# A two-layer gated MLP on one core: lo parts moved from GpSimd to VectorE, row sums spread over the groups

## The chip, the core and the metric

The kernel runs on one core of a Trainium2 chip. The metric is the device time of one execution in microseconds; three runs of the kernel before gave a median of 1682.23 us (1680.01 to 1683.55). One further execution was taken with the hardware profiler; all rows below come from it.

The engines are named as in the profile: PE is TensorE's matmul, PEld its weight load, DVE is VectorE, ACT is ScalarE, POOL is GpSimd, SP is SyncE (which issues the DMAs).

## The reference

An attention with a small memory comes first, and its output x (4608 tokens, 512 features) goes through two MLPs, all in float32:

```python
x = _attn_ref(q, k, v, phi)                     # reshaped to 4608 x 512
g = np.maximum(0.01 * (h := x @ w_in), h);  x = g @ w_out           # first MLP, d_ff 2048
gate = 1.0 / (1.0 + np.exp(-(x @ w_gate)))      # second MLP, d_ff 1536
val = x @ w_val
out = gate * val @ w_out
```

The change touches the second MLP alone, which takes the second half of the time.

## The kernel before

**Number format.** A float32 operand is held as two parts of a shorter type for TensorE: hi, a rounded copy made by ScalarE, and lo, the rest (operand minus hi), made by a subtraction on VectorE or GpSimd. A product of two such operands is three matmuls: hi*hi, hi*lo and lo*hi.

**Tiling of the second MLP.** Tokens are taken in five *pairs* of blocks: four pairs of 2 x 512 tokens and one of 2 x 256 (`PAIRS`). The 12 chunks of 128 hidden features are taken in three *thirds* of four chunks (index `th`), so there are 15 thirds in all, 12 full and 3 short ones. A third consists of four *groups* in the order gate, value, gate, value (indices `j` and `val` of `m2_group`), and then of the output products (`m2_out`). So in a third there is one place where a value group is followed directly by a gate group; behind the second value group stand the output products.

**A group.** Two blocks of tokens by two chunks of features are multiplied by the seven-product scheme of Winograd: seven products, k = 0 to 6, each of six matmuls of 512 columns, into three PSUM banks: x (k = 0, 3), y (k = 1, 4, 6) and z (k = 2, 5). A later product of a bank adds to what is in it, so it may start only when the earlier content has been read. The reads, in order:

- k=0: ScalarE copies x to `tmp` (L839); k=1: VectorE adds y to it (L844); k=2: ScalarE copies z (L849).
- k=3: the first result (f,t) = (0,0) is in x; k=4: VectorE reads y (L858), adds the copy of z (L859), result (1,1); k=5: VectorE reads z (L863), result (0,1); k=6: VectorE reads y (L868), result (1,0).

For each result, `finish` is called. In a gate group it is a sigmoid on ScalarE (L824) into an `sg` tile. In a value group VectorE multiplies the gate with the value (L829), ScalarE casts the product row to its hi part in a `pt` tile (L831), and a subtraction makes the lo part (L833): on GpSimd, but for the result (1,0) of the last value group of a third, which is on VectorE.

**Row sums of the next pair.** The left operands of the seven products are differences of the token blocks. For each pair and each half `a` of the features there are four subtractions on VectorE (`x_sums`, L754, L755, L757, L758) from the loaded rows `xr` into `xt`. For the next pair they stand in its predecessor's second third (th = 1): four behind the first value group, four behind the second. The loads of `xr` are issued on SP's queue at the end of the first third's groups, ahead of its output products. Their hi and lo parts (L771 on ScalarE, L775 in turn on VectorE and GpSimd) are made during the output products of the last third.

**Order.** Every engine takes its instructions in the order in which the code writes them (`tc.manual_schedule`); there is no planner here. What the code writes first is first in the engine's queue, and the tile pools add the waits for data and for buffers.

Of the kernel before, what the change touches and what calls it, by code (L numbers as in the profile page):

```python
# [93 lines left out]
def tile_kernel(  # L94
# [13 lines left out]
    nc = tc.nc  # L108
# [44 lines left out]
    def f32(ap):  # L153
        return ap.bitcast(F32)
# [15 lines left out]
    class Piece:  # L170
        i = -1
# [570 lines left out]
    def x_load(n, c):  # L742
        t0, h = PAIRS[n]
        nc.sync.dma_start(out=xr[c][:, 0:2 * h], in_=x2s[:, c, t0:t0 + 2 * h])

    def x_parts(n, a):
        h = PAIRS[n][1]
        b = [xr[2 * a + e][:, i * h:(i + 1) * h] for e in range(2) for i in range(2)]
        return b, (xt[a][:, 0:h], xt[a][:, 512:512 + h], b[1], xt[2][:, a * 512:a * 512 + h])

    def x_sums(n, a, k):
        (b11, b12, b21, b22), (t1, t2, t3, t4) = x_parts(n, a)
        if k == 0:
            nc.vector.tensor_sub(t1, b12, b11)  # L754
            nc.vector.tensor_sub(t3, b22, b12)  # L755
        else:
            nc.vector.tensor_sub(t2, b22, t1)  # L757
            nc.vector.tensor_sub(t4, b21, t2)  # L758

    def x_operand(n, k, a):  # L760
        (b11, _, b21, b22), (t1, t2, t3, t4) = x_parts(n, a)
# [2 lines left out]
    def x_hi(n, k, a):  # L764
        if n == 0:
            i = 2 * k + a
            xo[k, a] = (
                wtile("win", [P, 2, 512], F32R, "xo") if i < SLOTS["win"]
                else p2[0].tile([P, 2, 512], F32R, tag="xo", name="xo", bufs=6)
            )  # L770
        nc.scalar.copy(xo[k, a][:, 0, :PAIRS[n][1]], x_operand(n, k, a))  # L771

    def x_lo(n, k, a, eng):
        t, h = xo[k, a], PAIRS[n][1]
        eng.tensor_sub(t[:, 1, :h], x_operand(n, k, a), f32(t[:, 0, :h]))  # L775

    def w_load():
        while w_free and w_next[0] < len(PAIRS) * NOPS // 2:
            m = w_next[0] % (NOPS // 2)
            t = w_at[w_next[0]] = w_free.pop(0)  # L780
            nc.sync.dma_start(out=f32(t), in_=gvs[:, 2 * m:2 * m + 2].rearrange("p o l a f -> p (o l a f)"))
            w_next[0] += 1
# [6 lines left out]
    def tmp(h):  # L789
        n_tmp[0] += 1  # L790
        return tmps[n_tmp[0] % len(tmps)][:, :h]

    sgs = {}

    def m2_group(n, th, j, val):
        h = PAIRS[n][1]
        o0 = n * NOPS + NOP * (TH * th + 2 * j + val)
        last = val and j == TH // 2 - 1  # L800

        def prod(k, bank, start):
            m, e = divmod(o0 + k, 2)
            w = w_at[m].rearrange("p (o l a f) -> p o l a f", o=2, l=2, a=2)[:, e]
            i = 0
            for a in range(2):
                x = xo[k, a]
                for l, r in ((0, 0), (1, 0), (0, 1)):

                    nc.tensor.matmul(  # L810
                        bank, w[:, l, a, :], x[:, r, :h], start=(start and i == 0), stop=(i == 5),
                        skip_group_check=not start,
                    )
                    i += 1
            if e == 1:
                w_free.append(w_at.pop(m))
                w_load()

        def sg_tile():
            return p2[0].tile([P, 512], F32, tag="sg", name="sg", bufs=5)[:, :h]  # L820

        def finish(f, t, c, psum=False):
            if not val:
                nc.scalar.activation(sgs[f, t] if psum else c, c, AF.Sigmoid)  # L824
                if not psum:
                    sgs[f, t] = c
                return
            s = sgs.pop((f, t))
            nc.vector.tensor_mul(s, s, c)  # L829
            d = pt[2 * (2 * j + f) + t]  # L830
            nc.scalar.copy(d[:, 0, :h], s)  # L831
            eng = nc.vector if last and (f, t) == (1, 0) else nc.gpsimd
            eng.tensor_sub(d[:, 1, :h], s, f32(d[:, 0, :h]))  # L833

        new = (lambda: tmp(h)) if val else sg_tile
        x = ps_h.tile([P, 512], F32, tag="h", name="ps_x")[:, :h]
        prod(0, x, True)
        s1 = tmp(h)
        nc.scalar.copy(s1, x)  # L839
        yield  # L840
        y = ps_a.tile([P, 512], F32, tag="a", name="ps_y")[:, :h]
        prod(1, y, True)
        u2 = new()
        nc.vector.tensor_add(u2, y, s1)  # L844
        yield
        z = ps_h.tile([P, 512], F32, tag="h", name="ps_z")[:, :h]
        prod(2, z, True)
        c = tmp(h)
        nc.scalar.copy(c, z)  # L849
        yield  # L850
        prod(3, x, False)
        if not val:
            sgs[0, 0] = sg_tile()
        finish(0, 0, x, True)
        yield
        prod(4, y, False)
        u3 = new()
        nc.vector.tensor_add(u3, y, s1)  # L858
        nc.vector.tensor_add(u3, u3, c)  # L859
        finish(1, 1, u3)  # L860
        yield
        prod(5, z, False)
        nc.vector.tensor_add(u2, z, u2)  # L863
        finish(0, 1, u2)
        yield
        prod(6, y, False)
        c21 = new()
        nc.vector.tensor_add(c21, y, s1)  # L868
        finish(1, 0, c21)
        yield  # L870

    def m2_out(n, th, between):
# [54 lines left out]
    with tc.manual_schedule():  # L927
# [109 lines left out]
        for group in SCHED["prologue"]:  # L1037
# [4 lines left out]
            for x in group.split():  # L1042
# [4 lines left out]
                else:  # L1047
                    n, u = x.split(".")
# [19 lines left out]
                fin()  # L1068

        early = {0: [(x_open, ())] + [(x_load, (0, c)) for c in range(KD)]}  # L1070
        for n in range(4):
            early.setdefault(3 + n, []).append((x_sums, (0, n // 2, n % 2)))
        for n in range(2 * NOP):
            early.setdefault(6 + n, []).append((x_hi, (0, n // 2, n % 2)))
            early.setdefault(7 + n, []).append((x_lo, (0, n // 2, n % 2, nc.vector)))
# [7 lines left out]
        for n in range(TH):  # L1083
            early.setdefault(18 + 2 * n, []).append((w2_load, (n, n)))
        first = m2_group(0, 0, 0, 0)
        held = None
        for i, (b, hf, fc) in enumerate(steps):
# [47 lines left out]
        for n in range(len(PAIRS)):  # L1135
            more = n + 1 < len(PAIRS)
            for th in range(NTH):
                for j in range(TH // 2):
                    for val in range(2):
                        g = m2_group(n, th, j, val)  # L1140
                        if (n, th, j, val) == (0, 0, 0, 0):
                            g = first
                        for _ in g:
                            pass
                    if more and th == 1:
                        x_sums(n + 1, j, 0)
                        x_sums(n + 1, j, 1)
                if n + 1 < len(PAIRS) and th == 0:
                    for c in range(KD):
                        x_load(n + 1, c)  # L1150
                between = []
                if more and th == NTH - 1:
                    ops = [(k, a) for k in range(NOP) for a in range(2)]
                    for i in range(0, len(ops), 2):
                        fs = [lambda o=o: x_hi(n + 1, *o) for o in ops[i:i + 2]]
                        fs += [lambda o=o, e=e: x_lo(n + 1, *o, e) for o, e in zip(ops[i:i + 2], (nc.vector, nc.gpsimd))]
                        between.append(fs)
                    for f in between.pop(0):
                        f()
                m2_out(n, th, between)  # L1160
                if n + 2 == len(PAIRS) and th == NTH - 1:
                    w_free.extend(p2[0].tile([P, 2 * PC], F32R, tag="xr", name="wt", bufs=7) for _ in xr + xt)
                    w_load()
# [30 lines left out]
```

## Time and profile before

| | |
|---|---|
| median of 3 runs | 1682.23 us |
| the profiled execution | 1682.42 us, its span 1680.6 us |
| mean granted TensorE clock | 0.987 |
| PE busy / PEld busy | 1614.4 us (96%) / 1391.9 us (83%) |
| DVE busy | 831.0 us (49%) |
| ACT busy | 679.3 us (40%) |
| POOL busy | 581.9 us (35%) |
| chain that ended last | PE 52%, DVE 5%, ACT 1%; output products (L883) 17%, products (L810) 26% |
| lo parts of the product rows (L833) | 105 on POOL, mean 1405 ns; 15 on DVE, mean 896 ns |

A busy share says how much an engine has to do over the whole span; what a change in one place is worth has to be read at that place: which engine waits there, and for which instruction. So the rows below are mostly timelines, which list an engine's instructions in order of time, with the idle time before each and what ended it.

### The profile page before, as it was taken

Reading aid. Unit: us, or ns where it says so; the run is one execution under the profiler, and the core shown is the slowest. Engines: PE = TensorE matmul, PEld = TensorE weight load, DVE = VectorE, ACT = ScalarE, POOL = GpSimd, SP = SyncE. Lnnn points to the kernel's source line nnn. Section 1 sums busy time; section 2 is a strip of 40 time slices with the busy share of each in tenths; the row PEclk is TensorE's granted clock in tenths of the full one; section 3 lists DMA queues with packets and bytes.
Section 4 is the critical chain, followed back from the end, with each engine's and each line's share of the span. In section 5 each row is a group of like instructions: output and inputs, shape, how many; then the busy total and the mean of one; then the engine's idle time right before and its main releaser. Section 6 shows DMA issues by size and latency. Waiting matters only on the chain.

```text
span 1680.6 us, 26242 instructions
## 1 busy us (share of the span) xinstructions
PE 1614.4 (96%) x9976; PEld 1391.9 (83%) x9976; DVE 831.0 (49%) x1362; ACT 679.3 (40%) x1516; POOL 581.9 (35%) x534
## 2 busy tenths in 40 slices
PE   4688999999999999999999999999999999999998
PEld 2577888989898898989988788878887888878897
DVE  6997545454454544523142555264543454264544
ACT  4654455555455555544432133232332142222332
POOL 2776343444444354433321124121321142121311
PEclk8799999999999999999999999999999999999999
DMA  9712353444445353512465375554575456546692
GB/s 295 259 44 75 104 164 112 135 145 146 133 146 170 117 165 92 168 43 78 140 193 196 92 223 190 184 177 151 161 239 163 137 171 214 167 126 201 211 392 74
DMA packets 169022, 268.59 MB, mean 160 GB/s; under 512 B 60608, under 2 KB 105664, under 8 KB 168896
## 3 DMA queue, kind: packets, MB, share of 16 engines
q1 hardware_dynamic: 168896, 266.91, 50.1%
q8 instruction: 79, 1.29, 0.3%
q14 instruction: 47, 0.39, 0.1%
HBM read 219.68 MB, written 47.19 MB: 159 GB/s over the span
## 4 chain that ended last, share of the span: by engine, by line
PE 52%; DVE 5%; issue 1%; ACT 1%; DMA 0%; DVEq 0%; ACTq 0%; SPq 0%
PE oacc L883 17%; PE ps_y L810 11%; PE ps_x L810 8%; PE ps_z L810 7%; PE acc L700 5%; PE ps_h L678 3%; DVE sg L829 2%; DVE tmp L859 1%; DVE tmp L858 1%; PE ps_vw L651 0%; DVE tmp L868 0%; DVE tmp L863 0%; ACT tmp L839 0%; DVE xt L754 0%; DVE xr L755 0%
## 5 line engine op out<-in xcount | busy, mean ns | idle before, releaser
L700 PE MATMUL acc<-gh,wo 128*128 128x288 f32 x2048 | 434.6, 304 | 0.3 <-ACT gh L160 0.3
L833 POOL TENSOR_TENSOR pt<-sg,pt 128x512 fp32r<-128x512 f32 (+1 forms) x105 | 146.0, 1405 | 639.7 <-ACT pt L831 586.5
L700 PEld LDWEIGHTS acc<-gh,wo 128*128 128x128 f32 x2048 | 326.9, 189 | 37.4 <-ACT gr L683 19.5
L161 POOL TENSOR_TENSOR gl<-gr,gh 128x288 fp32r<-128x288 f32 x250 | 221.7, 890 | 334.7 <-ACT gh L160 210.8
L700 PE MATMUL acc<-gl,wo 128*128 128x288 f32 x1024 | 304.2, 297 | 1.3 <-POOL gl L161 1.3
L883 PE MATMUL oacc<-w2t,pt 128*128 128x512 f32 x1296 | 296.3, 389 | 0.0
L883 PEld LDWEIGHTS oacc<-w2t,pt 128*128 128x128 f32 x1296 | 243.1, 188 | 50.3
L810 PE MATMUL ps_y<-xo,wt 128*128 128x512 f32 (+1 forms) x1080 | 255.1, 372 | 9.1 <-DVE sg L844 9.1
L683 ACT ACTIVATE gr<-ps_h 128x288 f32<-128x288 f32 x256 | 105.4, 412 | 327.5 <-PE ps_h L678 299.7
L810 PEld LDWEIGHTS ps_y<-xo,wt 128*128 128x128 f32 x1080 | 191.7, 190 | 45.1 <-DVE sg L844 10.8
L678 PE MATMUL ps_h<-at_hi,vw 128*128 128x288 f32 x1024 | 213.7, 297 | 8.5 <-ACT vw L160 6.6
L700 PEld LDWEIGHTS acc<-gl,wo 128*128 128x128 f32 x1024 | 193.8, 189 | 2.3 <-POOL gl L161 2.0
L678 PEld LDWEIGHTS ps_h<-at_hi,vw 128*128 128x128 f32 x1024 | 166.3, 190 | 9.6 <-ACT vw L160 7.5
L810 PE MATMUL ps_x<-xo,wt 128*128 128x512 f32 (+1 forms) x720 | 169.3, 370 | 3.2 <-ACT tmp L839 2.6
L810 PE MATMUL ps_z<-xo,wt 128*128 128x512 f32 (+1 forms) x720 | 167.7, 368 | 0.2 <-DMA wt<-gvs 0.2
L810 PEld LDWEIGHTS ps_x<-xo,wt 128*128 128x128 f32 x720 | 126.3, 188 | 30.8 <-ACT tmp L839 8.8
L678 PE MATMUL ps_h<-at_lo,vw 128*128 128x288 f32 x512 | 151.4, 296 | 0.0
L810 PEld LDWEIGHTS ps_z<-xo,wt 128*128 128x128 f32 x720 | 127.6, 189 | 23.0 <-DVE tmp L868 0.3
L831 ACT CAST pt<-sg 128x512 fp32r<-128x512 f32 (+1 forms) x120 | 69.4, 578 | 164.5 <-DVE sg L829 164.5
L161 DVE TENSOR_TENSOR vw<-ps_vw,vw 128x512 fp32r<-128x512 f32 x64 | 44.1, 691 | 182.4 <-ACT vw L160 182.4
L160 ACT CAST gh<-gr 128x288 fp32r<-128x288 f32 x256 | 111.8, 437 | 1.6
L678 PEld LDWEIGHTS ps_h<-at_lo,vw 128*128 128x128 f32 x512 | 97.1, 190 | 0.0
(157 smaller groups left out, 1790.9 us busy)
## 6 DMA issues: line engine op xcount, KB each, us to landing
wt<-gvs SPq DMA_DIRECT2D x210, 512.0 KB, 4.4
w2t<-w2s SPq DMA_DIRECT2D x60, 512.0 KB, 5.6
gvs<-hl SPq DMA_DIRECT2D x84, 256.0 KB, 2.3
x2s<-obuf SPq DMA_DIRECT2D x15, 576.0 KB, 3.6
win<-in_moe_w_in_dram SPq DMA_DIRECT2D x16, 512.0 KB, 8.6
wo_bits<-in_moe_w_out_dram SPq DMA_DIRECT2D x16, 512.0 KB, 8.6
xr<-x2s SPq DMA_DIRECT2D x16, 512.0 KB, 6.3
q<-in_q_dram SPq DMA_DIRECT2D x60, 128.0 KB, 5.2
```

The lines of the kernel that those rows point to most:

```text
L160: nc.scalar.copy(hi, raw)
L161: eng.tensor_sub(lo, raw, f32(hi))
L678: nc.tensor.matmul(p[:, :HALF], w, x, start=(n == 0), stop=(n == 3 * NG - 1))
L683: nc.scalar.activation(gr, p[:, :HALF], AF.Prelu, alpha=0.01)
L700: nc.tensor.matmul(a[d][:, :HALF], w[:, ds_], x, start=(open_ and n == 0), stop=(close and n == 2),)
L810: nc.tensor.matmul(bank, w[:, l, a, :], x[:, r, :h], start=(start and i == 0), stop=(i == 5), skip_group_check=not start,)
L829: nc.vector.tensor_mul(s, s, c)
L831: nc.scalar.copy(d[:, 0, :h], s)
L833: eng.tensor_sub(d[:, 1, :h], s, f32(d[:, 0, :h]))
L858: nc.vector.tensor_add(u3, y, s1)
L859: nc.vector.tensor_add(u3, u3, c)
L883: nc.tensor.matmul(bank[i], pt[2 * f + t][:, l, q * P:(q + 1) * P], w2t[f][:, r, :], start=(f == 0 and l + r == 0), stop=(f == TH - 1 and ...
```

## The change

`x_sums` makes one subtraction per call in place of two. In the main loop the eight subtractions for the next pair are no longer written behind the value groups of the second third; they are put on a list (`extra`), and each gate group of the second and third thirds takes one behind its third product and one behind its fourth. The order of the eight among themselves stays, and for the first pair (`early`) nothing moves.

In `finish`, the lo part is now always made by VectorE, and it is not written at once: it is put on a list (`later`), and what is on the list is written right behind the next read of a PSUM bank (`read`). For the last result of a group (`tail`) the cast too is put on the list: it is written behind the next group's read of x, and the lo part behind that group's read of y. At the end of a third the list is emptied at once. GpSimd keeps only its share of the hi/lo parts of the next pair's rows.

```diff
--- before.py
+++ after.py
@@ -750,12 +750,8 @@
 
     def x_sums(n, a, k):
         (b11, b12, b21, b22), (t1, t2, t3, t4) = x_parts(n, a)
-        if k == 0:
-            nc.vector.tensor_sub(t1, b12, b11)
-            nc.vector.tensor_sub(t3, b22, b12)
-        else:
-            nc.vector.tensor_sub(t2, b22, t1)
-            nc.vector.tensor_sub(t4, b21, t2)
+        out, x, y = ((t1, b12, b11), (t3, b22, b12), (t2, b22, t1), (t4, b21, t2))[k]
+        nc.vector.tensor_sub(out, x, y)
 
     def x_operand(n, k, a):
         (b11, _, b21, b22), (t1, t2, t3, t4) = x_parts(n, a)
@@ -791,6 +787,8 @@
         return tmps[n_tmp[0] % len(tmps)][:, :h]
 
     sgs = {}
+    later = []
+    extra = []
 
 
 
@@ -819,7 +817,16 @@
         def sg_tile():
             return p2[0].tile([P, 512], F32, tag="sg", name="sg", bufs=5)[:, :h]
 
-        def finish(f, t, c, psum=False):
+
+        def read(*ops):
+            for op in ops:
+                op()
+            ops = later[:]
+            later.clear()
+            for op in ops:
+                op()
+
+        def finish(f, t, c, psum=False, tail=False):
             if not val:
                 nc.scalar.activation(sgs[f, t] if psum else c, c, AF.Sigmoid)
                 if not psum:
@@ -828,45 +835,61 @@
             s = sgs.pop((f, t))
             nc.vector.tensor_mul(s, s, c)
             d = pt[2 * (2 * j + f) + t]
-            nc.scalar.copy(d[:, 0, :h], s)
-            eng = nc.vector if last and (f, t) == (1, 0) else nc.gpsimd
-            eng.tensor_sub(d[:, 1, :h], s, f32(d[:, 0, :h]))
+
+            def lo():
+                nc.vector.tensor_sub(d[:, 1, :h], s, f32(d[:, 0, :h]))
+
+            def hi():
+                nc.scalar.copy(d[:, 0, :h], s)
+                later.append(lo)
+
+            if tail:
+                later.append(hi)
+            else:
+                hi()
 
         new = (lambda: tmp(h)) if val else sg_tile
         x = ps_h.tile([P, 512], F32, tag="h", name="ps_x")[:, :h]
         prod(0, x, True)
         s1 = tmp(h)
-        nc.scalar.copy(s1, x)
+        read(lambda: nc.scalar.copy(s1, x))
         yield
         y = ps_a.tile([P, 512], F32, tag="a", name="ps_y")[:, :h]
         prod(1, y, True)
         u2 = new()
-        nc.vector.tensor_add(u2, y, s1)
+        read(lambda: nc.vector.tensor_add(u2, y, s1))
         yield
         z = ps_h.tile([P, 512], F32, tag="h", name="ps_z")[:, :h]
         prod(2, z, True)
         c = tmp(h)
-        nc.scalar.copy(c, z)
+        read(lambda: nc.scalar.copy(c, z))
+        if extra and not val:
+            extra.pop(0)()
         yield
         prod(3, x, False)
         if not val:
             sgs[0, 0] = sg_tile()
+        read()
         finish(0, 0, x, True)
+        if extra and not val:
+            extra.pop(0)()
         yield
         prod(4, y, False)
         u3 = new()
-        nc.vector.tensor_add(u3, y, s1)
+        read(lambda: nc.vector.tensor_add(u3, y, s1))
         nc.vector.tensor_add(u3, u3, c)
         finish(1, 1, u3)
         yield
         prod(5, z, False)
-        nc.vector.tensor_add(u2, z, u2)
+        read(lambda: nc.vector.tensor_add(u2, z, u2))
         finish(0, 1, u2)
         yield
         prod(6, y, False)
         c21 = new()
-        nc.vector.tensor_add(c21, y, s1)
-        finish(1, 0, c21)
+        read(lambda: nc.vector.tensor_add(c21, y, s1))
+        finish(1, 0, c21, tail=True)
+        while last and later:
+            read()
         yield
 
     def m2_out(n, th, between):
@@ -1068,8 +1091,8 @@
                 fin()
 
         early = {0: [(x_open, ())] + [(x_load, (0, c)) for c in range(KD)]}
-        for n in range(4):
-            early.setdefault(3 + n, []).append((x_sums, (0, n // 2, n % 2)))
+        for n in range(8):
+            early.setdefault(3 + n // 2, []).append((x_sums, (0, n // 4, n % 4)))
         for n in range(2 * NOP):
             early.setdefault(6 + n, []).append((x_hi, (0, n // 2, n % 2)))
             early.setdefault(7 + n, []).append((x_lo, (0, n // 2, n % 2, nc.vector)))
@@ -1142,12 +1165,10 @@
                             g = first
                         for _ in g:
                             pass
-                    if more and th == 1:
-                        x_sums(n + 1, j, 0)
-                        x_sums(n + 1, j, 1)
                 if n + 1 < len(PAIRS) and th == 0:
                     for c in range(KD):
                         x_load(n + 1, c)
+                    extra.extend(lambda a=a, k=i: x_sums(n + 1, a, k) for a in range(2) for i in range(4))
                 between = []
                 if more and th == NTH - 1:
                     ops = [(k, a) for k in range(NOP) for a in range(2)]
```

The place where a value group is followed by a gate group, in the second third of the first pair, on VectorE. Of the kernel before (L858 reads y for k=4 of the value group, L829 are the multiplications, the last L844 reads y for k=1 of the gate group):

```order
L858 TENSOR_TENSOR tmp<-ps_y,tmp 128x512
L859 TENSOR_TENSOR tmp<-tmp 128x512
L829 TENSOR_TENSOR sg<-sg,tmp 128x512
L863 TENSOR_TENSOR tmp<-ps_z,tmp 128x512
L829 TENSOR_TENSOR sg<-sg,tmp 128x512
L868 TENSOR_TENSOR tmp<-ps_y,tmp 128x512
L829 TENSOR_TENSOR sg<-sg,tmp 128x512
L754 TENSOR_TENSOR xt<-xr 128x512
L755 TENSOR_TENSOR xr<-xr 128x512
L757 TENSOR_TENSOR xt<-xr,xt 128x512
L758 TENSOR_TENSOR xt<-xr,xt 128x512
L844 TENSOR_TENSOR sg<-ps_y,tmp 128x512
```

Here the four sums stand between the last multiplication and the gate group's read of y. The same stretch of VectorE in the changed kernel, from the second operation of k=4 on (L840 is the lo part, L836 the multiplication, L860 the gate group's read of y, L754 a sum):

```order
L880 TENSOR_TENSOR tmp<-tmp 128x512
L836 TENSOR_TENSOR sg<-sg,tmp 128x512
L884 TENSOR_TENSOR tmp<-ps_z,tmp 128x512
L840 TENSOR_TENSOR pt<-sg,pt 128x512
L836 TENSOR_TENSOR sg<-sg,tmp 128x512
L889 TENSOR_TENSOR tmp<-ps_y,tmp 128x512
L840 TENSOR_TENSOR pt<-sg,pt 128x512
L836 TENSOR_TENSOR sg<-sg,tmp 128x512
L860 TENSOR_TENSOR sg<-ps_y,tmp 128x512
L840 TENSOR_TENSOR pt<-sg,pt 128x512
L754 TENSOR_TENSOR xt<-xr,xt 128x512 x2
L879 TENSOR_TENSOR sg<-ps_y,tmp 128x512
```

Two lo parts in these rows, and a third one (of the result of k=3) in front of the first row shown, stand ahead of the gate group's read of y; the fourth stands behind it, and two of the sums follow there.

ScalarE at the same kind of place, from the value group's two copies on (before: L831 the casts, L839 and L849 the copies of x and z, L824 the sigmoid):

```order
L839 COPY tmp<-ps_x 128x512
L849 COPY tmp<-ps_z 128x512
L831 CAST pt<-sg 128x512 x4
L839 COPY tmp<-ps_x 128x512
L849 COPY tmp<-ps_z 128x512
L824 ACTIVATE sg<-ps_x 128x512
L824 ACTIVATE sg<-sg 128x512 x3
```

and in the changed kernel (L843 the casts, L855 and L865 the copies, L831 the sigmoid):

```order
L855 COPY tmp<-ps_x 128x512
L865 COPY tmp<-ps_z 128x512
L843 CAST pt<-sg 128x512 x3
L855 COPY tmp<-ps_x 128x512
L843 CAST pt<-sg 128x512
L865 COPY tmp<-ps_z 128x512
L831 ACTIVATE sg<-ps_x 128x512
L831 ACTIVATE sg<-sg 128x512 x3
```

The last of the four casts has moved behind the gate group's copy of x.

## Rows read from the trace of the kernel before

**Rows 1.** The chain that ended last, output blocks: start, length, engine, tile, line
```profile
880.52 21.76 PE oacc L883 x96
...
945.04 21.76 PE oacc L883 x96
...
1005.33 21.76 PE oacc L883 x96
...
1556.77 21.76 PE oacc L883 x96
```

**Rows 2.** Waits of PE, second MLP: line, waited for, us in total, times, longest
```profile
PE ps_y L810 <- DVE sg L844: 9.1, 4, 2.5
PE ps_x L810 <- ACT tmp L839: 2.6, 11, 0.6
```

**Rows 3.** Timeline of PE, a gate group's products k=1 to 4: start, length, [idle before]
```profile
1047.33 1.52 PE L810 MATMUL ps_y<-xo,wt 128*128 128x512 f32 x6
1048.69 1.52 PE L810 MATMUL ps_z<-xo,wt 128*128 128x512 f32 x6
1050.37 1.66 PE L810 MATMUL ps_x<-xo,wt 128*128 128x512 f32 x6 [0.16 <-ACT tmp L839]
1051.86 1.54 PE L810 MATMUL ps_y<-xo,wt 128*128 128x512 f32 x6
```

**Rows 4.** Timeline of DVE, the value group before it, from k=4 on
```profile
1043.45 0.69 DVE L858 TENSOR_TENSOR tmp<-ps_y,tmp 128x512 f32<-128x512 f32 x1 [0.67 <-PE ps_y L810]
1044.25 1.17 DVE L859 TENSOR_TENSOR tmp<-tmp 128x512 f32<-128x512 f32 x1
1045.45 0.69 DVE L829 TENSOR_TENSOR sg<-sg,tmp 128x512 f32<-128x512 f32 x1
1046.06 0.68 DVE L863 TENSOR_TENSOR tmp<-ps_z,tmp 128x512 f32<-128x512 f32 x1
1046.78 0.69 DVE L829 TENSOR_TENSOR sg<-sg,tmp 128x512 f32<-128x512 f32 x1
1047.39 0.68 DVE L868 TENSOR_TENSOR tmp<-ps_y,tmp 128x512 f32<-128x512 f32 x1
1048.11 1.07 DVE L829 TENSOR_TENSOR sg<-sg,tmp 128x512 f32<-128x512 f32 x1
```

**Rows 5.** Timeline of ACT, the same stretch: last cast, copy of the gate group's x
```profile
1049.21 0.62 ACT L831 CAST pt<-sg 128x512 fp32r<-128x512 f32 x1 [1.08 <-DVE sg L829]
1049.74 0.58 ACT L839 COPY tmp<-ps_x 128x512 f32<-128x512 f32 x1
```

**Rows 6.** Timeline of PE behind the row sums, first pair: k=4 of the gate group
```profile
929.75 2.93 PE L810 MATMUL ps_y<-xo,wt 128*128 128x512 f32 x6 [2.53 <-DVE sg L844]
```

**Rows 7.** That stretch by windows: us; PE, PEld, DVE, ACT, POOL busy; PEclk; DMA
```profile
923.90:934.00 10.10, 7.41 (x26) 5.39 (x24) 6.84 (x8) 2.28 (x4) 3.32 (x2) 0.83 0.40 122
```

**Rows 8.** Timeline of DVE there: first and third row sum, the gate group's read of y
```profile
924.29 1.77 DVE L754 TENSOR_TENSOR xt<-xr 128x512 f32<-128x512 f32 x1
...
927.69 0.68 DVE L757 TENSOR_TENSOR xt<-xr,xt 128x512 f32<-128x512 f32 x1
...
929.01 0.68 DVE L844 TENSOR_TENSOR sg<-ps_y,tmp 128x512 f32<-128x512 f32 x1
```

**Rows 9.** Timeline of POOL there: three lo parts in one row of the timeline
```profile
922.12 5.10 POOL L833 TENSOR_TENSOR pt<-sg,pt 128x512 fp32r<-128x512 f32 x3 [2.06 <-issue]
```

**Rows 10.** Instructions on tile sg, VectorE: ns min/median/max of the lo parts
```profile
L833 DVE TENSOR_TENSOR pt<-sg,pt x15: 425/1012/1018, 884.2 to 1666.8; 128x512 fp32r<-128x512 f32 x12, 128x256 fp32r<-128x256 f32 x3
```

**Rows 11.** Timeline of DVE, a lo part of a token row, POOL idle
```profile
1022.30 0.68 DVE L775 TENSOR_TENSOR xo<-xt,xo 128x512 fp32r<-128x512 f32 x1
```

**Rows 12.** DMA issues of the next pair's rows: count, KB each, median us to landing
```profile
xr<-x2s SPq DMA_DIRECT2D x16, 512.0 KB, 6.3
```

**Rows 13.** Timeline of PE, a short third: k=2 and k=3 of its second gate group
```profile
1622.27 0.88 PE L810 MATMUL ps_z<-xo,wt 128*128 128x256 f32 x6
1623.73 0.98 PE L810 MATMUL ps_x<-xo,wt 128*128 128x256 f32 x6 [0.58 <-ACT tmp L839]
```

## The prediction, made before the changed kernel was run

> **What bounds the kernel now.** I read the chain of waits first. In the second MLP it runs along TensorE: the reader is to see output blocks of 21.76 us and, from one to the next, the length of a third [rows 1]. From 945.04 to 1005.33 that is 60.29 us, an ordinary third; from 880.52 to 945.04 it is 64.52 us, the one with the row sums. A product takes 1.36 us (1047.33 to 1048.69, [rows 3]), so 28 products and an output block without any wait are 38.08 + 21.76 = 59.84 us. The 11 thirds from 880.52 to 1556.77 took 676.25 us [rows 1]; 11 x 59.84 = 658.24, so 18.0 us are lost in them. An ordinary third loses 0.45; the very first one, ahead of the first row, I count with the same, so the twelve full thirds lose 18.46: 12 x 0.45 = 5.40 at an ordinary place, and the rest, 13.06, beside the sums of four pairs.
>
> The list of TensorE's waits names the two places [rows 2]: L810 on a copy by ScalarE (L839) and, four times and longest, on VectorE's read of y (L844).
>
> The ordinary place is the step from a value group to the next gate group, and the timelines of three engines show it. The gate group's product k=3 was due at 1048.69 + 1.36 = 1050.05, started at 1050.37, and the one behind it came 1.49 later in place of 1.36 [rows 3]: 0.32 + 0.13 = 0.45. It waited for ScalarE's copy of x (1049.74 to 1050.32), which stands in ScalarE's queue behind the cast at 1049.21 [rows 5], and that waited for VectorE's last multiplication, 1048.11 + 1.07 [rows 4]. VectorE had worked through seven operations without a gap since 1043.45.
>
> At the sums the same queue is longer: the first sum takes 1.77 us, and the gate group's read of y starts only at 929.01 [rows 8]. TensorE sat idle for 2.53 us, and the product behind took 2.93 us [rows 6] against 1.52. In that stretch the granted clock was 0.83 [rows 7], so part of it ran at the lower of the two levels, 1.2 GHz in place of 2.4; a wait there can cost more than its idle time.
>
> **The change part by part.** Prices: a VectorE operation on 512 columns takes 0.69 us; the next one starts 0.61 later, or 0.72 if it reads the result (1045.45, 1046.06, 1046.78, [rows 4]). A cast takes 0.62 [rows 5]; from the end of a multiplication to its cast, and of a copy to TensorE, pass some 0.04 (1048.11 + 1.07 against 1049.21; 1050.32 against 1050.37).
>
> *Lo parts on VectorE.* A lo part was shown on VectorE with 425 ns at least and 1.01 us mostly [rows 10], with GpSimd at work beside it; the same subtraction for a token row with GpSimd idle took 0.68 [rows 11]. The low end for 512 columns is that 0.68, the high end 1.02. I take 0.69, because GpSimd has nothing left to do in the groups. Likewise L859 (1.17) and the last multiplication (1.07) [rows 4], and the first sum (1.77): all ran while GpSimd made lo parts (five microseconds from 922.12, [rows 9]), and the third sum, the same kind of operation when GpSimd was through, took 0.68 [rows 8]. So I take 0.69 for these too; if the price is the operand's own they stay.
>
> The Trainium skill, "GPSIMD Engine Reference", section "Key points", says that GpSimd shares its SBUF interfaces with VectorE and that VectorE instructions with two SBUF inputs suffer. By that page the prices fall to 0.69 and the sum is the one below; without it, with the slow prices left as they are, it is that of the second rival. This trace fits the page (1.77 against 0.68), but shows no value group with GpSimd idle.
>
> *The walk with these prices*, on the clock of [rows 4]: read of y 1043.45; lo of the k=3 result 44.06; L859 44.67; multiplication 45.39; read of z 46.00; its lo part has to wait for a cast that runs from 46.12 to 46.74, so 46.78; multiplication 47.39; read of y 48.00; lo part, again 0.17 late, 48.78; last multiplication 49.39; the gate group's read of y 50.00, done at 50.69. Queued behind each waiting lo part are the next multiplication and the reads of banks, and TensorE waits for those; that is in this walk. ScalarE's third cast ends at 48.74, the copy of x follows directly and is done by 49.33, where it was 50.32. Product k=3 is due at 50.05 and k=4, which needs the read of y, at 51.41. Both come 0.67 ahead; since a late release costs 0.13 beyond the wait, I count 0.5 of that as margin. So the wait at the ordinary place goes, and nothing takes its place: 12 x 0.45 = 5.40.
>
> *Sums.* Behind the read at 50.00 follow the fourth lo part, whose cast ends at 50.74: 50.78, and two sums, 51.39 and 52.00 to 52.69. The next read of y is for k=4, which ends at 51.41 + 1.52 = 52.93. So the sums lie in a gap of VectorE's and cost nothing; without that cover each would delay a read that TensorE needs at k=6, 2.72 us after k=4's start. Their rows are loaded in 6.3 us [rows 12], issued ahead of an output block of 21.76 us, so they lie ready although they are wanted a group earlier. The 13.06 us go, the lower clock with them.
>
> *End of a third.* The last lo part, cast included, ends at 51.47, which is 8.0 us after k=4's end. The output block begins 2.7 after k=4's end and reads that part only in its 30th matmul (29 x 21.76/96 = 6.6 later): 9.3. Covered, by 1.3.
>
> *The other engines.* VectorE takes over 105 subtractions, 72 us in all. In a value group it then has 13 operations, 0.61 to 0.72 apart, some 8.4 of 7 x 1.36 = 9.52 us: the fullest place, and the reason for the walk. ScalarE's work is the same, SP's queue keeps its order, GpSimd only loses work.
>
> *Short thirds.* TensorE's idle time at the same step is 1623.73 - 1622.27 - 0.88 = 0.58 [rows 13]. A short product takes about half, a VectorE operation 425 ns and not 345, and three more of them stand in the queue. Between nothing and 0.58 goes; I take half, 0.29 x 3 = 0.9.
>
> Sum: 18.46 + 0.9 = 19.4. The profiled execution took 1682.42 us (span 1680.6, and 1.8 around it), 0.2 from the median of the runs: 1663.0 us.
>
> **The rivals.** *The wait moves to the read of y.* If lo parts cost 1.02 and L859 stays at 1.17, the three lo parts and L859 bring the read 3 x 0.33 + 0.48 = 1.5 later; less 0.5 of margin, plus 0.13, TensorE waits 1.1 at k=4 in 12 thirds: 13 us back, 1676. If only half of that surcharge is real, the wait is 0.4 and the time 1668. For it: L859 was slow in the row shown, and its inputs are both `tmp`. Against: the operations on one `sg` and one `tmp` are 0.69 in the same rows unless GpSimd is well under way.
>
> *Slower: the sums in the gate groups.* If the slow price is the operand's own and the sums keep 1.77 too, then behind the late walk two sums start at 52.3 + 0.6 and end at 56.4; the read of y for k=4 ends at 57.1, while TensorE wants k=6 at 54.13 + 1.1. It waits 1.9 us more in each gate group behind a value group that carries sums, two for each of four pairs: 15 us on top of 13, and 1663 + 28 = 1691. It turns slower once the sums cost about 1.2 apiece with the lo parts at 1.02. Against it stands the third sum's 0.68.
>
> *The waits are not the bound.* If TensorE were held by something the list doesn't name, a third would not fall below 60.29 by filling these gaps: within 3 us of before, 1680. The 1.36 spacing elsewhere in the same rows speaks against it.
>
> **How the numbers follow.** The forecast gets 0.70 (1660.5 to 1666, if the short thirds gain all or nothing and the runs spread by some 2 us, as those of before did), the moved wait 0.18 (1667 to 1677), the unnamed bound 0.05, the slower case 0.07. The range goes from 1660 to 1672: the forecast and about half of the moved wait. What this kernel's measurement can tell from no change is about 0.2%, 3.4 us; faster than that are the first two, 0.88, the same 0.05, slower 0.07.
>
> **What the profile of the changed kernel would show.** Right: both lines of [rows 2] gone or under 1 us; all full thirds 59.8 to 59.9 apart, with and without sums; 120 lo parts on VectorE near 0.69, sums and L859 too; the granted clock 1.00 beside the sums. A wait of L810 on the read of y at k=4 would be the first rival, on the reads at k=6 the second. Lo parts near 1 us with GpSimd idle would make the prices wrong, and a third of 60.3 without any named wait the whole account.

## The result, and the profile after

The changed kernel took 1661.32 us (median; 1660.55 to 1661.53), the kernel before, on the same chip, 1682.32. The ratio of the two is 0.9876 (95% interval 0.9859 to 0.9893): 21 us less. Forecast was 1663.0, in 1660 to 1672. All rows below come from single profiled executions; that of the changed kernel took 1660.55 us, that of before 1682.42.

The page of the changed kernel: the span, the busy time of each engine, and the engines' shares of the chain that ended last.

```profile
span 1658.8 us, 26089 instructions
PE 1606.2 (97%) x9976; PEld 1390.8 (84%) x9976; DVE 853.0 (51%) x1467; ACT 681.1 (41%) x1516; POOL 434.6 (26%) x429
...
PE 58%; DMA 0%; DVE 0%; ACT 0%; issue 0%; SPq 0%; ACTq 0%
```

VectorE (DVE) is busier than before and GpSimd (POOL) idler, as the change says; but VectorE has left the chain, and that is what a reader should look for, not its busy share.

The list of TensorE's waits from 838 us on, which answers to [rows 2]. Both lines there are gone; the whole second MLP has one wait left, in the first short third:

```profile
PE ps_z L808 <- ACT pt L843: 0.3, 1, 0.3
```

The output blocks in the chain, which answer to [rows 1] (start, length):

```profile
878.38 21.76 PE oacc L906 x96
938.22 21.76 PE oacc L906 x96
998.06 21.76 PE oacc L906 x96
...
1536.62 21.76 PE oacc L906 x96
1579.58 10.91 PE oacc L906 x48
1611.19 10.91 PE oacc L906 x48
1642.80 10.92 PE oacc L906 x48
```

From 878.38 to 938.22 (a third with sums, 64.52 before) and from 938.22 to 998.06 (an ordinary one, 60.29 before) it is 59.84 us each. The 11 thirds up to 1536.62 take 658.24 us, 11 x 59.84 to the hundredth.

VectorE's timeline at the ordinary place, which answers to [rows 4]; it begins one row later, with the value group's read of y for k=4, and ends with the gate group's read of y:

```profile
1036.18 0.69 DVE L879 TENSOR_TENSOR tmp<-ps_y,tmp 128x512 f32<-128x512 f32 x1 [0.67 <-PE ps_y L808]
1036.79 0.68 DVE L840 TENSOR_TENSOR pt<-sg,pt 128x512 fp32r<-128x512 f32 x1
1037.39 0.68 DVE L880 TENSOR_TENSOR tmp<-tmp 128x512 f32<-128x512 f32 x1
...
1042.09 0.69 DVE L836 TENSOR_TENSOR sg<-sg,tmp 128x512 f32<-128x512 f32 x1
1042.69 0.68 DVE L860 TENSOR_TENSOR sg<-ps_y,tmp 128x512 f32<-128x512 f32 x1
```

L880 takes 0.68 (it was 1.17), the last multiplication 0.69 (1.07), and the gate group's read of y (L860) starts 6.51 us behind the first row; the walk had said 6.55.

Beside the sums of the first pair, which answers to [rows 8]: the gate group's read of y, the fourth lo part, two sums in one row, the read of y for k=4.

```profile
923.01 0.68 DVE L860 TENSOR_TENSOR sg<-ps_y,tmp 128x512 f32<-128x512 f32 x1
923.78 0.69 DVE L840 TENSOR_TENSOR pt<-sg,pt 128x512 fp32r<-128x512 f32 x1
924.39 1.41 DVE L754 TENSOR_TENSOR xt<-xr,xt 128x512 f32<-128x512 f32 x2
926.02 0.69 DVE L879 TENSOR_TENSOR sg<-ps_y,tmp 128x512 f32<-128x512 f32 x1 [0.22 <-PE ps_y L808]
```

The two sums fit, and VectorE then waits 0.22 us for TensorE, not the other way round. The clock there, in the columns of [rows 7]:

```profile
922.00:929.00 7.00, 7.00 (x33) 5.79 (x32) 5.92 (x10) 3.19 (x6) 0.00 (x0) 1.00 0.62 178
```

1.00 in place of 0.83, and TensorE busy throughout.

**Where the 21.9 us between the two profiled executions are:** 18.0 in the 11 thirds; 1.4 in the short thirds (1536.62 to 1642.80 is 106.18, before 107.59); 2.1 ahead of the first output block (880.52 against 878.38); 0.3 behind the last one and around the span. Of the 2.1, 0.45 is the first third's ordinary wait. The other 1.7 lies before the second MLP, where nothing was changed: VectorE's first read of y there starts at 841.7 before and 840.0 after, and in the eight kernels of the experiments it starts anywhere from 840.1 to 841.8. I count it as spread between executions and no part of the change.

### The profile page after: what moved, and what is told of

It is laid out like the page before. It is cut to its first block, busy times and chain, and to the rows that moved or that the text cites. A ratio compares the mean times of both kernels' runs of the same rounds, so it can differ in the third digit from the quotient of the medians.

```text
span 1658.8 us, 26089 instructions
## 1 busy us (share of the span) xinstructions
PE 1606.2 (97%) x9976; PEld 1390.8 (84%) x9976; DVE 853.0 (51%) x1467; ACT 681.1 (41%) x1516; POOL 434.6 (26%) x429
## 3 DMA queue, kind: packets, MB, share of 16 engines
q8 instruction: 79, 1.29, 0.3%
## 4 chain that ended last, share of the span: by engine, by line
PE 58%; DMA 0%; DVE 0%; ACT 0%; issue 0%; SPq 0%; ACTq 0%
PE oacc L906 18%; PE ps_y L808 13%; PE ps_z L808 9%; PE ps_x L808 9%; PE acc L700 6%; PE ps_h L678 3%; PE ps_vw L651 0%; DMA gvs<-hl 0%; PE ps_kv L502 0%; PE ps_sc L567 0%; DVE hl L298 0%; PE ps_qT L550 0%; DVE st L603 0%; ACT e L596 0%; DVE osum L917 0%
## 5 line engine op out<-in xcount | busy, mean ns | idle before, releaser
L771 POOL TENSOR_TENSOR xo<-xr,xo 128x512 fp32r<-128x512 f32 (+1 forms) x16 | 23.0, 1460 | 671.0 <-ACT xo L767 671.0
L843 ACT CAST pt<-sg 128x512 fp32r<-128x512 f32 (+1 forms) x120 | 69.6, 580 | 182.1 <-DVE sg L836 182.1
```

## The experiments

The change has three parts: spread sums, lo parts on VectorE, and a late last cast, with each lo part a bank read after its cast. The first four kernels take them apart.

**Sums alone** (cast and lo part as before, together and on GpSimd; sums spread):

```
-            if tail:
-                later.append(hi)
-            else:
-                hi()
+            nc.scalar.copy(d[:, 0, :h], s)
+            eng = nc.vector if last and (f, t) == (1, 0) else nc.gpsimd
+            eng.tensor_sub(d[:, 1, :h], s, f32(d[:, 0, :h]))
```

> Only the spreading of the row sums is kept; casts and lo parts stand as in the kernel before (lo on GpSimd, the last cast ahead of the gate group's copy of x). Theory (a queue account with prices set by GpSimd being busy): the sums no longer stand ahead of the gate group's read of y, so 13 us go, and the 0.45 us at each of 12 ordinary places stays, the 0.6 of short thirds too: all full thirds 60.3 apart, some 1668.5 us in all. Rival (the sums are dear by themselves, 1.77 us wherever they stand): two of them delay the gate group's read for k=4, thirds with sums stay 0.6 or more longer than 60.3, 1672 us or more.

Measured 1669.42 us, ratio 0.9928 (0.9913 to 0.9942). Its waits of TensorE, and its first three output blocks:

```profile
PE ps_x L808 <- ACT tmp L847: 2.9, 13, 0.6
```

```profile
879.54 21.76 PE oacc L898 x96
939.87 21.76 PE oacc L898 x96
1000.21 21.76 PE oacc L898 x96
```

60.33 both times: the third with sums has become an ordinary one, and the ordinary wait stayed. Its short thirds stayed at 32.26 too. The spread sums alone save 12 us.

**Sums back** (as the changed kernel, the sums again behind the value groups):

```
+                    if more and th == 1:
+                        for k in range(4):
+                            x_sums(n + 1, j, k)
-                    extra.extend(lambda a=a, k=i: x_sums(n + 1, a, k) for a in range(2) for i in range(4))
```

> Only the sums go back to their old place behind the value groups; lo parts on VectorE and the late last cast stay. Theory: ordinary thirds stay at 59.84; with GpSimd idle a sum takes 0.69, four of them put the gate group's read of y some 2.7 us later, of which 0.6 is margin: TensorE waits about 2.1 us at k=4 in three thirds and about 1 in that of the short pair, thirds with sums near 62, and 1.4 more where the clock falls: 1668 to 1672 us. Rival (the sums' 1.77 is their own price): a wait of 4 us, thirds near 64.5, 1675 us or more.

Measured 1671.61, ratio 0.9938 (0.9923 to 0.9953). VectorE's timeline at the sums, and TensorE's product behind:

```profile
923.88 0.68 DVE L754 TENSOR_TENSOR xt<-xr 128x512 f32<-128x512 f32 x1
924.60 0.69 DVE L754 TENSOR_TENSOR xr<-xr 128x512 f32<-128x512 f32 x1
925.21 1.41 DVE L754 TENSOR_TENSOR xt<-xr,xt 128x512 f32<-128x512 f32 x2
```

```profile
927.27 1.67 PE L808 MATMUL ps_y<-xo,wt 128*128 128x512 f32 x6 [1.78 <-DVE sg L860]
```

The four sums take 0.68 to 0.70 each with GpSimd idle, 1.77 and 1.67 for the first two before. The queue is still too long by 1.78 us where they stand together, so cheap sums are not enough; they have to lie in a gap. A third with sums takes 61.95 us, 2.11 over 59.84: the product is 1.93 late (due 1.36 after the one at 923.98) and 0.18 more is lost behind it. That makes 7.4 in its profiled execution (three such and one of 1.04); the median over the runs is 10.3 above the changed kernel. The profiled one was the shortest run, 1668.45, and where the longer ones lost the rest no trace shows.

**Lo parts on GpSimd** (the changed kernel's order, lo parts on GpSimd):

```
-                nc.vector.tensor_sub(d[:, 1, :h], s, f32(d[:, 0, :h]))
+                eng = nc.vector if last and (f, t) == (1, 0) else nc.gpsimd
+                eng.tensor_sub(d[:, 1, :h], s, f32(d[:, 0, :h]))
```

> Only the engine of the lo parts goes back: GpSimd makes them as before, in the changed order (last cast behind the gate group's copy of x, sums spread). Theory: what held TensorE was the order in ScalarE's and VectorE's queues, so the late cast alone frees the copy of x, and the prices of VectorE go back to 1.17 and 1.07 without reaching the path: thirds of 59.8 to 59.9, 1661 to 1663 us. Rival (the lo parts have to leave GpSimd for the gain): VectorE stays slow beside GpSimd, waits at k=4 or k=6 come back, thirds at 60.3 or more, 1666 us or more.

Measured 1661.68, ratio 0.9884 (0.9868 to 0.9901): the changed kernel's time. All full thirds are 59.84 and the short ones 31.4, 0.2 less than the changed kernel's. Yet VectorE is slow again:

```profile
921.68 1.07 DVE L836 TENSOR_TENSOR sg<-sg,tmp 128x512 f32<-128x512 f32 x1
...
923.28 2.88 DVE L754 TENSOR_TENSOR xt<-xr,xt 128x512 f32<-128x512 f32 x2
926.62 0.69 DVE L880 TENSOR_TENSOR sg<-ps_y,tmp 128x512 f32<-128x512 f32 x1 [0.46 <-PE ps_y L808]
```

The two sums take 2.88 us and still end 0.46 before the read behind them can start. So moving the lo parts to VectorE is not what gives the gain: the slow prices are real, but where they fall in this order they are covered.

**No late cast** (the changed kernel, the last cast written at once):

```
-        finish(1, 0, c21, tail=True)
+        finish(1, 0, c21)
```

> Only the late last cast is undone: the cast of a group's last result is written at once, the lo parts stay on VectorE, one bank read behind, the sums stay spread. Theory: the copy of x stands behind that cast again, and VectorE now reaches the last multiplication 1.3 us later than before, so TensorE waits 1.24 us at k=3 and loses 1.4 with the late start: 12 full thirds at 61.2, some 1678 us, most of the gain gone. Rival (the lead of the VectorE prices is what matters, the cast's place is worth little): under 0.5 us per third, 1667 us or less.

Measured 1680.03, ratio 0.999 (0.9981 to 1.0). TensorE at the ordinary place:

```profile
1047.22 1.52 PE L808 MATMUL ps_z<-xo,wt 128*128 128x512 f32 x6
1049.76 1.65 PE L808 MATMUL ps_x<-xo,wt 128*128 128x512 f32 x6 [1.02 <-ACT tmp L855]
```

The product k=3 was due at 1047.22 + 1.36 = 1048.58 and came 1.18 late, every third 61.16 in place of 59.84. With the lo parts on VectorE and the last cast ahead of the copy of x, nearly the whole gain is gone: VectorE's longer queue makes the copy later than it was before the change.

**Late cast alone** (lo parts on GpSimd, sums at their old place), the counterpart: both edits of *Lo parts on GpSimd* and *Sums back* together.

> Of the change only the late last cast is kept: lo parts on GpSimd, the sums back behind the value groups. Theory (two separate waits, each with its own remedy): ordinary thirds at 59.84, so 5.4 us less, 0.6 to 0.8 less in each short third; beside the sums the read of y for k=1 is as late as in the kernel before, so TensorE waits the longer there by what the other wait gave, thirds with sums 62.9 or, where the clock falls, 64.3: 1672 to 1677 us. Rival (the two remedies need each other): under 3 us gained, 1679 us or more.

Measured 1679.48, ratio 0.9993 (0.9983 to 1.0002): missed. Ordinary thirds are at 59.84 and short ones at 31.4, as expected. But the thirds with sums take 64.70, 64.72, 64.74 and 63.64, where before they took 64.52, 63.11, 64.44 and 62.08. TensorE behind the sums, and the clock there:

```profile
929.31 2.50 PE L808 MATMUL ps_y<-xo,wt 128*128 128x512 f32 x6 [2.98 <-DVE sg L861]
931.61 2.31 PE L808 MATMUL ps_z<-xo,wt 128*128 128x512 f32 x6
```

```profile
925.00:929.00 4.00, 1.33 (x6) 0.75 (x5) 3.93 (x5) 1.18 (x2) 1.78 (x2) 1.00 0.68 212
929.00:934.00 5.00, 4.69 (x14) 3.72 (x15) 1.69 (x4) 0.50 (x1) 0.00 (x0) 0.66 0.08 31
```

Without the wait at k=3, TensorE reaches the product behind the sums earlier and waits 2.98 us for the same queue, in place of 2.53 [rows 6]. The product was due 1.36 after the one that started at 924.81, so it is 3.14 late; behind it the clock is at its lower level, 1.2 GHz, for part of two products, which take 2.30 and 2.14 from start to start (the next one starts at 933.75) in place of 1.36: another 1.72. Together that is the 4.86 of this third. In the 12 full thirds the excess over 59.84 is 18.4 us (4.86 + 4.88 + 4.90 + 3.80), and before it was 18.46: all of what the ordinary places gained was given back at the sums, and the 2 us that remain are the short thirds. The two remedies are worth 12 and 2 alone and 21 together; each makes the other's wait the last one.

**Lo part at once** (sums spread; cast and lo part on VectorE directly behind each multiplication, no bank read between them):

```
-            def hi():
-                nc.scalar.copy(d[:, 0, :h], s)
-                later.append(lo)
...
+            nc.scalar.copy(d[:, 0, :h], s)
+            nc.vector.tensor_sub(d[:, 1, :h], s, f32(d[:, 0, :h]))
```

> Lo parts on VectorE, each written right behind its cast and no cast late: the deferral by a bank read is undone, the engine and the spread sums stay. Theory (VectorE's queue is strictly in order): every lo part holds VectorE through its cast, so that a multiplication and its lo part take 1.39 us from start to start in place of 0.61; the last lo part of a value group ends near 8.9 us after the end of k=4, the copy of x waits behind the cast, TensorE waits 2.3 at k=3: 12 thirds near 62.2, about 1690 us, slower than the kernel before. Rival (the place of the cast is all, the lo parts' waits are hidden): as with the late cast alone undone, 1680 us.

Measured 1730.84, ratio 1.029 (1.0275 to 1.0306): the direction was right, the size was not. VectorE's waits, TensorE's products, and the clock:

```profile
DVE pt L840 <- ACT pt L839: 77.2, 120, 0.7
```

```profile
1057.64 1.52 PE L808 MATMUL ps_z<-xo,wt 128*128 128x512 f32 x6
1061.43 2.91 PE L808 MATMUL ps_x<-xo,wt 128*128 128x512 f32 x6 [2.27 <-ACT tmp L846]
1064.13 1.90 PE L808 MATMUL ps_y<-xo,wt 128*128 128x512 f32 x6
```

```profile
1055.00:1059.00 4.00, 4.00 (x19) 3.12 (x17) 2.77 (x5) 1.10 (x2) 0.00 (x0) 1.00 0.60 162
1059.00:1066.00 7.00, 4.73 (x14) 3.68 (x14) 2.50 (x4) 2.19 (x4) 0.00 (x0) 0.76 0.32 83
```

Each lo part waits about 0.69 us for its cast, as expected. What I had missed stands in the other rows: product k=3, due at 1059.00, starts at 1061.43, and then it and the next run partly at the lower clock, 1.34 and 0.38 longer than at full clock (2.70 and 1.74 from start to start, against 1.36; the one behind them starts at 1065.87). With the 2.43 of lateness, 0.3 at k=6 of each of the two value groups and 0.3 in the output block that makes the 5.1 that this third takes over 59.84 (its blocks start 64.96 apart). The three short thirds lose another 9.7 together. This kernel differs from *No late cast* in the place of the lo part alone: placing it one bank read later is worth 51 us (1730.84 against 1680.03), once it is on VectorE. The late cast brings another 19 in this order, down to 1661.32.

**GpSimd kept busy** (the changed kernel, and GpSimd repeats each lo part into a scratch tile that nobody reads). It asks whether GpSimd's work is what makes VectorE's operations slow:

```
+                nc.gpsimd.tensor_sub(scratch[0][:, :h], s, f32(d[:, 0, :h]))
```

> The changed kernel, and GpSimd makes each lo part a second time into a scratch tile that nobody reads (work added; nothing of the result changes). Theory (VectorE is slowed by GpSimd's subtractions): lo parts on VectorE near 1 us and L859's counterpart near 1.17 while GpSimd works, the gate group's read of y some 1 to 1.5 us later, TensorE waits 0.5 to 1.1 at k=4 in 12 thirds: 1667 to 1676 us. Rival (the prices belong to operands or places, not to GpSimd): lo parts stay at 0.69, 1661 us.

Measured 1724.25, ratio 1.025 (1.0233 to 1.0267): the cause is confirmed, the size missed by far. The expected wait for the gate group's read of y is there, 0.9 at most, but I had not seen that two others would come up, for ScalarE's copy of x and, the largest, in the output block for a cast:

```profile
PE oacc L911 <- ACT pt L844: 16.2, 12, 1.4
PE ps_x L809 <- ACT tmp L860: 12.0, 15, 1.0
PE ps_y L809 <- DVE sg L865: 11.9, 15, 0.9
```

VectorE, then GpSimd, at the ordinary place:

```profile
1052.62 0.69 DVE L884 TENSOR_TENSOR tmp<-ps_y,tmp 128x512 f32<-128x512 f32 x1 [0.67 <-PE ps_y L809]
1053.23 1.35 DVE L841 TENSOR_TENSOR pt<-sg,pt 128x512 fp32r<-128x512 f32 x1
...
1056.59 0.69 DVE L841 TENSOR_TENSOR pt<-sg,pt 128x512 fp32r<-128x512 f32 x1
1057.20 1.78 DVE L837 TENSOR_TENSOR sg<-sg,tmp 128x512 f32<-128x512 f32 x1
```

```profile
1052.74 1.29 POOL L848 TENSOR_TENSOR scr<-sg,pt 128x512 f32<-128x512 f32 x1 [18.93 <-ACT pt L844]
1056.70 1.74 POOL L848 TENSOR_TENSOR scr<-sg,pt 128x512 f32<-128x512 f32 x1 [2.67 <-ACT pt L844]
```

The reader is to compare ends. GpSimd's operations end at 1054.03 and 1058.44, the VectorE operations that started beside them at 1054.58 and 1058.98: 0.55 and 0.54 later. The trace of before has the same: L859 ends at 1044.25 + 1.17 = 1045.42 [rows 4], beside a GpSimd operation of this row:

```profile
1043.58 1.30 POOL L833 TENSOR_TENSOR pt<-sg,pt 128x512 fp32r<-128x512 f32 x1 [21.95 <-ACT pt L831]
```

It ends at 1044.88, 0.54 earlier. These rows are typical: in the second MLP all 81 VectorE operations on 512 columns of two SBUF tiles that start beside a GpSimd operation end 0.55 to 0.56 after it in the trace of before, and all 99 end 0.55 after it in this one. So a slow price is no property of the operation: it lasts until GpSimd is done. And in reverse: the second GpSimd operation, which started 0.11 behind a lo part on VectorE, took 1.74 in place of 1.29; the first, beside a read of a bank (one SBUF operand), was not held.

**GpSimd, half the columns**, to tell "until GpSimd is done" from a surcharge on each VectorE operation:

```
+                nc.gpsimd.tensor_sub(scratch[0][:, :h // 2], s[:, :h // 2], f32(d[:, 0, :h // 2]))
```

> The changed kernel with GpSimd repeating each lo part into a scratch tile that nobody reads, but on half the columns. Theory, formed from the run with all columns (a VectorE subtraction or product of two SBUF tiles that begins beside a GpSimd one is held until that one ends, and ends 0.54 us behind it): GpSimd's operation takes 0.75 to 0.9, so the multiplications behind lo parts take 0.8 to 0.95 in place of 1.78, the gate group's read of y is 0.3 to 0.7 later: 1661 to 1667 us. Rival (a fixed surcharge of some 1.1 us for each such meeting): 1.78 as with all columns, 1715 to 1725 us.

Measured 1677.55, ratio 0.9978 (0.9969 to 0.9988), above the theory's 1661 to 1667 and far below the rival's 1715 to 1725. VectorE and GpSimd:

```profile
1044.23 1.23 DVE L837 TENSOR_TENSOR sg<-sg,tmp 128x512 f32<-128x512 f32 x1
...
1046.76 1.23 DVE L837 TENSOR_TENSOR sg<-sg,tmp 128x512 f32<-128x512 f32 x1
```

```profile
1040.32 0.74 POOL L848 TENSOR_TENSOR scr<-sg,pt 128x256 f32<-128x256 f32 x1 [19.45 <-ACT pt L844]
1043.73 1.18 POOL L848 TENSOR_TENSOR scr<-sg,pt 128x256 f32<-128x256 f32 x1 [2.67 <-ACT pt L844]
1046.26 1.19 POOL L848 TENSOR_TENSOR scr<-sg,pt 128x256 f32<-128x256 f32 x1 [1.34 <-ACT pt L844]
```

The same multiplication takes 1.23 in place of 1.78, and again ends 0.55 and 0.54 behind GpSimd's (1045.46 against 1044.91, 1047.99 against 1047.45). A fixed surcharge is ruled out. The time was missed because I had taken GpSimd's half operation at its free length: it took 1.18 where it started beside VectorE, against 0.74 free. With the multiplications at 1.23, the gate group's read of y came 1.2 later than in the changed kernel, where I had expected 0.3 to 0.7. GpSimd's 0.44 more is the same as with all columns (0.45): a fixed delay behind a VectorE operation that still had some 0.6 to run, and not a slower pace.

The Trainium skill, "SBUF — State Buffer", section "Who interferes with whom", has a rule for this: a VectorE instruction with two SBUF inputs contends with a GpSimd instruction that reads SBUF, the port pair that they share is an exclusive lock, and the order of issue decides who blocks. These rows agree in both directions.

## Why the prediction was right

- **The bound.** Right. TensorE with no wait gives 59.84 us to a third, and 11 of 11 took that. The rival that something unnamed holds TensorE is out.
- **Ordinary places, 5.40.** Right in size: 0.45 each went, and the walk over VectorE's queue held to within 0.05 us. *No late cast* shows which part does it: with the cast ahead of the copy of x the wait is 1.18 and not 0.
- **Sums, 13.06.** Right: the four thirds with sums came down to 59.84, the clock to 1.00. *Sums alone* shows it apart from the rest (12 us).
- **Short thirds, 0.9.** Mis-sized: 1.4. The term took half of the 0.58 us of idle time [rows 13] three times. Measured: 0.65 in two of them (32.26 to 31.61), most of what the late product k=3 had cost; with the lo parts left on GpSimd 0.83 went (31.43). In the first it was 0.1 (43.06 to 42.96): there the one wait left, 0.3, stands.
- **Prices with GpSimd idle, 0.69.** Right: 120 lo parts on VectorE with a median of 0.691 us and none above 0.695 (24 of them are short), L880 and the sums too.
- **What these prices are worth.** The prediction let the forecast hang on them, and made their failing the rival of 1668 to 1676. The forecast did not need them: if lo parts stay on GpSimd in the new order, L859's counterpart and the last multiplication are as slow as before and do no harm (*Lo parts on GpSimd*, 1661.68). So the time came out right without the part of the change that the title names first; the order gives it. And the 1.02 of [rows 10], which the rival took for the lo part's own price, is no price of an operation: it depends on when GpSimd's ends. Where GpSimd worked in the same places (*GpSimd kept busy*) a lo part took 1.35 and a multiplication 1.78, with a time of 1724, far past that rival; lo parts at 1.02 with GpSimd idle, the rival's own case, occur in no run.
- **The lower clock.** I had said that a wait can cost more than its idle time. It does. My expectation for *Lo part at once* priced idle time alone; that for *Late cast alone* did have the lower clock as a case, a third of 64.3, but the clock fell at all four places, and the three full ones took 64.7.
- **Not predicted:** the 1.7 us ahead of the second MLP. With the 0.5 more of the short thirds and the 0.3 at the end they bring the profiled execution to 21.9 in place of the 19.4 worked out, and I hold them for spread.

## What to carry to other kernels

Where one engine feeds TensorE in order, walk its queue instruction by instruction: the gain came from what stands ahead of a read that TensorE waits for (a cast moved behind a copy, sums put into gaps), and a faster instruction was worth nothing where it was covered. Two waits along one chain are not additive: with one gone the other grows, so alone each remedy brought 2 and 12 us and both brought 21. Before work is put on GpSimd, look which VectorE operations with two SBUF inputs will start beside it: each is held until GpSimd's ends.

## What the runs showed of the hardware

- VectorE's operations with two SBUF inputs that started beside a GpSimd subtraction ended 0.54 to 0.56 us after it, whatever its length (1.29, 1.74 and 1.18 us; 81 of 81 on 512 columns in the second MLP of the kernel before). On 256 columns it was 0.28 to 0.30 there, 20 of 20. GpSimd's operations, started beside one of VectorE's, were 0.44 to 0.45 longer at 512 and at 256 columns. Reads of a bank on VectorE stayed at 0.68 to 0.69.
- After each of three waits of 1.78 us (*Sums back*, in the one execution profiled), TensorE's next products kept the full clock (1.67 and 1.55 us); after waits of 2.27 and 2.98 they ran in part at 1.2 GHz, and each time some 1.7 us more were lost by it. The same was lost after a wait of 1.91 at the fourth pair's sums in *Late cast alone* (granted clock 0.71 in the 5.9 us behind it). Of three waits of 2.53 to 2.54 in the kernel before, two were followed by a product of 2.93 us and one by 1.66. So the length of the wait alone does not tell whether the clock falls; what else does is open.
- A product released late is followed by the next 0.13 to 0.18 us later than the wait alone explains (1.49 in place of 1.36 from start to start after a wait of 0.16 us [rows 3]). This was read off, and its cause not tried.
